# The first 512 tokens of an attention-and-MLP kernel: row norms by TensorE products, first k and v ahead of the weights

## The chip, the cores and the metric

The kernel runs on one core of a Trainium2 chip. Times are device microseconds (us) of that core; a kernel's time is the median of several executions. The engines are named TensorE (PE, with its weight loads as PEld), VectorE (DVE), ScalarE (ACT), GpSimd (POOL) and SyncE (SP). ACT, POOL and SP also issue DMAs here, each into a queue of its own.

## What is computed

Linear attention without softmax, a row norm with a gain, and an MLP with a leaky ReLU on its output. `B, H, S, D` are 8, 8, 576, 64; the MLP sees 4608 tokens of width 512 and has 2048 hidden units.

```python
kv  = np.einsum('bhsd,bhse->bhde', k, v)
out = np.einsum('bhsd,bhde->bhse', q, kv)
rms = np.sqrt(np.mean(out * out, axis=-1, keepdims=True) + 1e-06)
x   = (out / rms * g_norm)        # then (B,H,S,D) -> (B*S, H*D)
h   = x @ w_in
g   = np.maximum(0.01 * h, h)
y   = g @ w_out
```

q, k, v and g_norm are float32; the two weight matrices arrive as 64-bit floats and are rounded to float32 on the chip.

## The kernel before, in words

The tokens are cut into nine blocks of 512 (`NT`). `x` is held transposed, features on the partitions: `x[:, 2*l + e, :]` is a tile of 128 partitions by 512 tokens, and a head's 64 features are spread over two halves `e` of 32 partitions (`E`). Four groups of 32 partitions (`NP`) are the four head pairs `p`, and `l` picks one of the two heads of a pair.

The first block is made by `first_attention` and worked off by `first_block`; the other eight blocks run later with products that save multiplications (`strassen`, `product_h`, `product_o`), which the change doesn't touch.

*Loads.* `load_first` issues q, k and v of the first batch: one DMA of 288 KB for each head pair of each, through the queues "a" (ACT), "s" (SP) and "g" (POOL). Some of them land in the buffers `pairs` and `early`, which are used for something else later. Each of the 32 weight jobs (`load_w`) brings 0.5 MB of 64-bit floats into one of seven raw buffers (three in `stage`, four in `pairs`): a `w_in` job is four DMAs of 128 KB, a `w_out` job is one of 512 KB. Job 0 goes through POOL's queue, all others through SP's. After it POOL issues four small DMAs for the gain `g_sb`. A queue issues in order: a DMA that waits for a buffer or for its semaphore (eight are used in turn) holds back what stands behind it.

*Rounding.* `round_f64` (L201) takes two instructions on ScalarE (L214 "add", L216 "cut") and four on VectorE (L217, L220, L221, L223), all on 128x512. Job 0 is the first slice of `w_in`; jobs 1 and 2 are the next of `w_in` and the first of `w_out`.

*first_attention* (L391): q is turned by small products with `ident` (q_ps, rest_ps) and copied to `qT` by ScalarE and VectorE; `attention_kv` makes k-transposed-times-v in two groups of head pairs, m = 0 (pairs 0 and 1) and m = 1 (pairs 2 and 3), 36 products each; `copy_kv` moves the result to SBUF. `keep_warm` issues products of zeros whose result nobody reads. Then the 512 tokens are done in two halves of 256. For each half, `outputs` makes 16 products into PSUM tiles `o_ps`, squares them on ScalarE, adds the two halves `e` on VectorE, and writes `x` with the gain (ScalarE, L317). `divide` (L326) sums the squares over 32 partitions and spreads the root's inverse again over them: VectorE turns 32x32 squares (L331), reduces (L332), ScalarE takes the root (L334), VectorE the reciprocal (L335), ScalarE repeats each value 32 times (L338), VectorE turns back (L341) and multiplies `x` (L343). Between the halves stand four keep_warm products. Afterwards jobs 1 to 4 are rounded.

*first_block* (L747): for each of 16 slices of 128 hidden units (n = 0 to 15), four products of 128x512 make `h_ps` (for n = 0 in two halves of 256 tokens), ScalarE's leaky ReLU (L765) makes `g`, and four products add to the output sums `o_acc`; the h products of n + 1 run ahead of the o products of n. Between them `between` loads and rounds further jobs and takes steps of the next batch's attention.

The instructions that carry `pin` stay in the order in which they are written; every matmul goes through L112, and every load of q, k, v here through L124, of the weights through L192.

Of the kernel before, what the change touches and what calls it, by code (L numbers as in the profile page):

```python
# [9 lines left out]
F32 = mybir.dt.float32  # L10
U32 = mybir.dt.uint32
I64 = mybir.dt.int64
# [11 lines left out]
def kernel(  # L24
# [36 lines left out]
    nc = tc.nc  # L61
# [37 lines left out]
    def view(t, lo, *shape):  # L99
        n = 1  # L100
        for d in shape:
            n *= d
        t = t[:, lo:lo + n]
        names = "abcd"[:len(shape)]
        return t.rearrange(f"p ({' '.join(names)}) -> p {' '.join(names)}",
                           **dict(zip(names, shape))) if len(shape) > 1 else t
# [4 lines left out]
    def matmul(*args, **kw):  # L111
        pin(nc.tensor.matmul(*args, **kw))  # L112
# [4 lines left out]
    def half_of(p, i):  # L117


        return i ^ (p & 1)  # L120
# [23 lines left out]
    def load_first():  # L144

        early = xpool.tile([P, NE * NT], F32, tag="xT", name="early")
        n = J * D

        def rows(t):
            return t[:, :n].rearrange("p (j d) -> p j d", j=J)  # L150

        ks, vs = ([in_tile(name) for _ in range(2)] for name in ("k", "v"))
        qs = [rows(ins.tile([P, T * D], F32, tag="q_in", name="q_in")) for _ in range(2)]
        qs += [rows(early[:, i * n:]) for i in range(2)]
        ks, vs = (t + [pair(i + j, J, D) for i in range(2)] for j, t in ((0, ks), (2, vs)))
        for way, to, src, ts, p in (
                ("a", q_ins, q, qs, 0), ("s", q_ins, q, qs, 1), ("a", q_ins, q, qs, 2),
                ("s", q_ins, q, qs, 3), ("a", k_ins, k, ks, 0), ("s", v_ins, v, vs, 0),
                ("a", k_ins, k, ks, 1), ("s", v_ins, v, vs, 1), ("g", k_ins, k, ks, 2),
                ("g", v_ins, v, vs, 2), ("s", k_ins, k, ks, 3), ("s", v_ins, v, vs, 3)):  # L160
            to[0, p] = load_two({"a": nc.scalar, "s": nc.sync, "g": nc.gpsimd}[way],
                                src[0, 2 * p:2 * p + 2], ts[p])

    kvs = [consts.tile([P, NP, D], F32, name=f"kv_{i}") for i in range(2)]
    zeros = view(g_all[0], 0, NT)
    load_first()
    nc.vector.memset(zeros, 0.0)

# [30 lines left out]
    def round_f64(dst, raw):  # L201

        a, n = dst.shape[1:]
        lo, hi = raw[:, :, 0], raw[:, :, 1]
        add = spare(a * n, "add", U32)
        pin(nc.scalar.activation(add, lo, func=AF.Copy, scale=2.0 ** -29))  # L214
        cut = spare(a * n, "cut")
        pin(nc.scalar.activation(cut, hi.bitcast(F32), func=AF.Copy, scale=2.0 ** -112))  # L216
        pin(nc.vector.tensor_scalar(cut, cut, HIGH_MOST, -HIGH_MOST, op0=ALU.min, op1=ALU.max))  # L217
        dst = dst.bitcast(U32)
        add, cut = (t.rearrange("p (a n) -> p a n", a=a) for t in (add, cut.bitcast(U32)))
        pin(nc.vector.tensor_scalar(dst, cut, 3, None, op0=ALU.logical_shift_left))  # L220
        pin(nc.vector.scalar_tensor_tensor(dst, in0=cut, scalar=0x80000000, in1=dst,  # L221
                                           op0=ALU.bitwise_and, op1=ALU.bitwise_or))
        pin(nc.vector.tensor_tensor(dst, dst, add, op=ALU.add))  # L223

    w_in_e = w_in.rearrange("(p t i) f -> p i t f", p=NP, i=E)
# [11 lines left out]
    def load_w(j, eng=nc.sync):  # L237
# [3 lines left out]
        else:  # L241
            load(dst, src, eng)

    def round_w(j):
        if w_in.dtype == I64:
            round_f64(w_jobs[j][0], w_raws.pop(j))

    eps_sb = consts.tile([P, 1], F32, name="eps_sb")
    nc.vector.memset(eps_sb, EPS)
    warm = consts.tile([P, 1], F32, name="warm")  # L250
    nc.scalar.activation(warm, eps_sb, func=AF.Sqrt)
    ident = consts.tile([P, P], F32, name="ident")
    nc.gpsimd.memset(ident, 1.0)
    nc.gpsimd.affine_select(ident, ident, pattern=[[-1, P]], base=0, channel_multiplier=1,
                            compare_op=ALU.is_equal, fill=0.0)
    load_w(0, nc.gpsimd)
    g_sb = consts.tile([P, 2], F32, name="g_sb")
    for p in range(NP):
        pin(nc.gpsimd.dma_start(g_sb[p * E:(p + 1) * E], g_norm.rearrange("(e i) -> i e", i=E)))


    xTs = {}
# [8 lines left out]
    def attention_kv(b, m, kv_ps):  # L271

        two = [(k_ins.pop((b, p)), v_ins.pop((b, p)), p) for p in (2 * m, 2 * m + 1)]
        for j in range(J):
            for i in range(2):
                for k_in, v_in, p in two:
                    r, c = 64 * i, 64 * half_of(p, i)
                    matmul(kv_ps[p % 2][c:c + 64, m, :], lhsT=k_in[r:r + 64, j, :],
                           rhs=v_in[r:r + 64, j, :], start=(j == 0), stop=(j == J - 1))
# [12 lines left out]
    def x_of(lo, hi):  # L292
        return block(lo // NT)[:, :, lo % NT:lo % NT + hi - lo]

    def outputs(b, lo, hi, e, sums, new_ps, new=t2k, later=None):


        x, n = x_of(lo, hi), hi - lo
        o_ps = [new_ps(n, "o_ps") for _ in range(2)]
        for p in range(NP):  # L300
            for l in range(2):
                r = slice(64 * l, 64 * l + 64)
                matmul(o_ps[half_of(p, l)][E * p:E * p + E, :], lhsT=kvs[b % 2][r, p, E * e:E * e + E],
                       rhs=qTs[b][r, p, lo - b * S:hi - b * S], start=True, stop=True)
        for l in range(2):
            sq = new(n, "sq" if e else f"sum{l}")
            act = nc.scalar.activation(sq, o_ps[l], func=AF.Square)
            if later is not None:
                pin(act)
            if e == 0:  # L310
                sums.append(sq)
            else:
                nc.vector.tensor_add(sums[l], sums[l], sq)

        def keep():
            for l in range(2):
                act = nc.scalar.activation(x[:, 2 * l + e, :], o_ps[l], func=AF.Copy,  # L317
                                           scale=g_sb[:, e:e + 1])
                if later is not None:
                    pin(act)  # L320
        if later is None:
            keep()
        else:
            later.append(keep)

    def divide(lo, hi, sums, new=t2k):  # L326
        x, n = x_of(lo, hi), hi - lo
        rms = work.tile([P, 2, n // E], F32, tag="rms", name="rms", bufs=2)
        for l in range(2):
            t = new(n, "turned")  # L330
            nc.vector.transpose(t, sums[l])  # L331
            nc.vector.tensor_reduce(rms[:, l, :], t.rearrange("p (a i) -> p a i", i=E),  # L332
                                    axis=AX.X, op=ALU.add)
        nc.scalar.activation(rms, rms, func=AF.Sqrt, scale=1.0 / D, bias=eps_sb)  # L334
        nc.vector.reciprocal(rms, rms)  # L335
        for l in range(2):
            t = new(n, "spread")
            nc.scalar.copy(t.rearrange("p (a i) -> p a i", i=E),  # L338
                           rms[:, l, :].unsqueeze(2).to_broadcast([P, n // E, E]))
            inv = new(n, "inv")  # L340
            nc.vector.transpose(inv, t)  # L341
            to = x[:, 2 * l:2 * l + 2, :]
            nc.vector.tensor_mul(to, to, inv.unsqueeze(1).to_broadcast([P, 2, n]))  # L343

    def att_ps(n, name):
        return ps_att.tile([P, n], F32, tag="att", name=name)

    def tail_of(b, lo, hi):
        sums = []
        for e in range(2):  # L350
            outputs(b, lo, hi, e, sums, att_ps)
            yield
        divide(lo, hi, sums)
        yield
# [36 lines left out]
    def first_attention():  # L391
# [4 lines left out]
        def keep_warm(n=1):  # L396
            for _ in range(n):
                matmul(idle, lhsT=zeros[:, :P], rhs=zeros, start=True, stop=True)
# [19 lines left out]
        for i in range(2):  # L418
            nc.vector.tensor_copy(
                qT.rearrange("p a (t j) -> p a t j", j=J)[:, i::2, :, J - 1], rest[i])  # L420
        for m in range(2):
            attention_kv(0, m, kv_ps)
            if m == 0:
                keep_warm()
        copy_kv(0, kv_ps)
        for j in range(3, 7):
            load_w(j)
        round_w(0)
        free = iter(("ha", "hb", "hc", "oa", "hd", "oc", "ha", "hb"))

        def ps(n, name):
            return ps_m.tile([P, n], F32, tag=next(free), name=name)

        sums, later = ([], []), []
        for e in range(2):
            outputs(0, 0, N2, e, sums[0], ps, spare, later)
        for keep in later:
            keep()
        outputs(0, N2, NT, 0, sums[1], ps, spare)
        divide(0, N2, sums[0], spare)  # L440
        outputs(0, N2, NT, 1, sums[1], ps, spare)

        idle = att_ps(NT, "idle_ps")
        keep_warm(4)
        divide(N2, NT, sums[1], spare)
        for j in range(1, 5):
            round_w(j)

# [450 lines left out]
```

## Time and profile before

| what | value |
|---|---|
| median of 6 executions | 942.69 us (941.35 to 944.72) |
| the profiled execution | 941.35 us, its span 939.6 us |
| granted TensorE clock, mean | 0.997 |
| DMA | 200.03 MB, mean 213 GB/s |
| first product of zeros; first q product; first kv product | 1.53; 5.24; 9.97 us |
| first square; first h product (half the tokens); first full-width h product | 20.34; 26.72; 34.50 us |
| ScalarE square of 128x256; ReLU of 128x512 | 0.39 to 0.41; 0.60 us |
| VectorE turn, reduction, product with x (128x256, 128x256, 128x512) | 0.42; 0.39; 0.66 us |

The page's first part gives each engine's busy time and share. The second cuts the span into 40 slices of 23.5 us, too coarse for a change that lies within the first 35 us; so the timeline (instructions in order of time), the chain of waits and tables of one microsecond each are read for that stretch. A TensorE product of f32 is recorded as two matmuls. The span leaves out what lies around the program's own work: here 1.75 us.

### The profile page before, as it was taken

To read this page: it belongs to the slowest core of one execution; us is meant where nothing else is said; L and a number is where in the kernel's file an instruction comes from. 1 tells how busy PE (TensorE), PEld (TensorE's weight loads), DVE (VectorE), ACT (ScalarE), POOL (GpSimd) and SP (SyncE) were. 2 spreads that over 40 slices of the span, in tenths; PEclk is the share of its full clock that TensorE was granted. 3 is DMA by queue.
4 is the path that set the end of the run, shared out by engine and by line. 5 is a ranking of instruction groups with operands and counts; after the bars stand their busy time and mean duration, and the time that the engine had idled before them with its cause. 6 is when DMAs were issued, how large, how long until landed. Compare 5 with 4: busy or idle time off the path is not lost.

```text
span 939.6 us, 17607 instructions
## 1 busy us (share of the span) xinstructions
PE 918.6 (98%) x6878; PEld 769.8 (82%) x6878; DVE 600.1 (64%) x1001; ACT 330.8 (35%) x671; POOL 319.4 (34%) x320
## 2 busy tenths in 40 slices
PE   7899999999999999999999999999999999999997
PEld 4444446878988899889998999899988999999996
DVE  3876895678357755597547855785568755554554
ACT  3643633242134422442234323432344233223321
POOL 2000253977622352216211722263224522532222
PEclk9999999999999999999999999999999999999999
DMA  8999925985498568955896678857855665567632
GB/s 248 218 247 224 252 75 164 328 270 173 159 309 268 163 186 260 308 182 179 247 306 202 185 257 259 250 169 219 271 177 175 198 218 183 182 195 221 188 112 90
DMA packets 89810, 200.03 MB, mean 213 GB/s; under 512 B 9856, under 2 KB 41600, under 8 KB 89728
## 3 DMA queue, kind: packets, MB, share of 16 engines
q1 hardware_dynamic: 79392, 187.17, 66.2%
q10 hardware_dynamic: 9856, 10.62, 3.5%
q8 instruction: 55, 0.90, 0.4%
q0 software_dynamic: 480, 1.12, 0.4%
q14 instruction: 27, 0.22, 0.1%
HBM read 172.39 MB, written 26.48 MB: 212 GB/s over the span
## 4 chain that ended last, share of the span: by engine, by line
PE 87%; DVE 7%; DMA 3%; ACT 2%; issue 1%; SPq 0%; ACTq 0%; DVEq 0%
PE o_a L112 21%; PE o_c L112 16%; PE h_ha L112 10%; PE h_hc L112 8%; PE h_hb L112 7%; PE h_hd L112 6%; PE o_acc L112 5%; PE h_ps L112 5%; PE h_a L112 3%; DVE g L451 2%; PE h_c L112 2%; PE o_ps L112 2%; PE kv_ps L112 2%; DMA pairs<-in_v_dram 1%; DVE o L451 1%
## 5 line engine op out<-in xcount | busy, mean ns | idle before, releaser
L451 POOL TENSOR_TENSOR gs<-g 128x512 f32<-128x512 f32 x64 | 80.3, 1274 | 450.4 <-ACT g L623 450.4
L451 DVE TENSOR_TENSOR o<-o_c,o 128x512 f32<-128x512 f32 x88 | 60.5, 688 | 111.8 <-PE o_c L112 107.8
L112 PE MATMUL o_a<-pairs,gs 128*128 128x256 f32 x512 | 121.1, 379 | 0.0
L451 DVE TENSOR_TENSOR o<-o_a,o 128x512 f32<-128x512 f32 x104 | 71.1, 684 | 77.2 <-PE o_a L112 77.2
L687 ACT COPY w_all<-h_ha 128x512 f32<-128x512 f32 x84 | 48.8, 581 | 200.6 <-PE h_ha L112 200.4
L623 ACT ACTIVATE g<-g 128x512 f32<-128x512 f32 x124 | 77.4, 631 | 99.9 <-DVE g L451 97.4
L112 PEld LDWEIGHTS o_a<-pairs,gs 128*128 128x128 f32 x512 | 93.0, 190 | 10.3
L112 PE MATMUL o_a<-w,g 128*128 128x256 f32 x256 | 61.0, 381 | 3.8 <-DVE o L451 3.6
L112 PEld LDWEIGHTS h_ha<-stage,w_all 128*128 128x128 f32 x448 | 58.0, 191 | 7.0 <-issue 2.4
L112 PE MATMUL h_ps<-xT,w_all 128*128 128x512 f32 (+1 forms) x136 | 58.3, 571 | 3.9 <-DVE xT L343 3.0
L112 PE MATMUL o_c<-w,g 128*128 128x256 f32 x256 | 60.5, 379 | 0.0
L112 PE MATMUL o_c<-pairs,gs 128*128 128x256 f32 x256 | 60.5, 379 | 0.0
L112 PE MATMUL o_c<-w,gs 128*128 128x256 f32 x256 | 60.5, 379 | 0.0
L112 PE MATMUL o_a<-pairs,g 128*128 128x256 f32 x256 | 60.5, 379 | 0.0
L112 PE MATMUL h_ha<-stage,w_all 128*128 128x128 f32 x448 | 60.1, 277 | 0.0
L112 PE MATMUL o_acc<-w,g 128*128 128x512 f32 x128 | 58.0, 597 | 0.0
L112 PEld LDWEIGHTS o_a<-w,g 128*128 128x128 f32 x256 | 46.4, 190 | 10.1 <-DVE o L451 3.5
L451 POOL TENSOR_TENSOR pairs<-w_all 128x512 f32<-128x512 f32 x8 | 10.5, 1314 | 126.2 <-DMA stage<-in_moe_w_out_dram 95.2
L112 PEld LDWEIGHTS h_ps<-xT,w_all 128*128 128x128 f32 x136 | 25.3, 190 | 33.6 <-issue 26.3
L451 DVE TENSOR_TENSOR g<-g,pairs 128x512 f32<-128x512 f32 x84 | 52.8, 682 | 0.0
L451 DVE TENSOR_TENSOR w_all<-h_hc,w_all 128x512 f32<-128x512 f32 x56 | 38.4, 686 | 21.7 <-PE h_hc L112 18.5
L112 PEld LDWEIGHTS o_c<-w,gs 128*128 128x128 f32 x256 | 46.5, 190 | 5.2
(152 smaller groups left out, 1977.2 us busy)
## 6 DMA issues: line engine op xcount, KB each, us to landing
w_all<-w SPq DMA_DIRECT2D x196, 448.0 KB, 4.0
pairs<-w SPq DMA_DIRECT2D x56, 512.0 KB, 4.4
out_dram<-o ACTq DMA_DIRECT2D x36, 256.0 KB, 2.9
v_in<-in_v_dram SPq DMA_DIRECT2D x30, 288.0 KB, 6.7
k_in<-in_k_dram SPq DMA_DIRECT2D x28, 288.0 KB, 6.0
q_in<-in_q_dram SPq DMA_DIRECT2D x56, 144.0 KB, 6.2
q_in<-in_q_dram SPq DMA_DIRECT2D x56, 140.0 KB, 5.9
w<-stage SPq DMA_DIRECT2D x12, 512.0 KB, 3.5
```

What stands on the lines that cost most here:

```text
L112: pin(nc.tensor.matmul(*args, **kw))
L451: ins = eng.tensor_tensor(out_, a, b_, op=ALU.subtract if minus else ALU.add)
L623: nc.scalar.activation(t, t if src is None else src, func=AF.Prelu, alpha=SLOPE)
L687: nc.scalar.copy(q[:, at], banks[tag])
```

## The change

- The order of the first loads and their queues. k and v of pair 1 move from ACT and SP to POOL; k of pair 3 moves from SP to ACT; `ident` is made between POOL's two pairs of loads. The four `g_sb` DMAs move from POOL to SP.
- `round_f64` becomes a generator, and job 0's four VectorE instructions are issued between others.
- One keep_warm product now stands ahead of each group of kv products; the four later ones are gone.
- For the first 512 tokens `outputs` and `divide` are replaced. All 32 `o_ps` products are issued together; a square covers 128x512 (both `e`). The sum over partitions is a product: the squares are the weights (128 tokens at a time), and the moving operand is `group`, 128x4, the identity summed over groups of 32 columns. It gives tokens on the partitions. ScalarE takes the root, VectorE the reciprocal, and a second product spreads it: the weights are one column of the roots repeated 32 times, the moving operand is `ident`; the result `inv_ps` stays in PSUM, and VectorE multiplies `x` by it. The first half's products with the gain move from ScalarE to VectorE.
- The tokens 512 to 575 of the first batch and all later batches keep the old way (`tail_of`).

```diff
-                ("a", k_ins, k, ks, 1), ("s", v_ins, v, vs, 1), ("g", k_ins, k, ks, 2),
-                ("g", v_ins, v, vs, 2), ("s", k_ins, k, ks, 3), ("s", v_ins, v, vs, 3)):
+                ("g", k_ins, k, ks, 1), ("g", v_ins, v, vs, 1), ("a", k_ins, k, ks, 3),
+                ("s", v_ins, v, vs, 3), ("g", k_ins, k, ks, 2), ("g", v_ins, v, vs, 2)):
+            if (way, p) == ("g", 2) and src is k:
+                make_ident()
...
+    group = consts.tile([P, NP], F32, name="group")
+    nc.vector.tensor_reduce(group, ident.rearrange("p (a i) -> p a i", i=E), axis=AX.X, op=ALU.add)
     load_w(0, nc.gpsimd)
...
-        pin(nc.gpsimd.dma_start(g_sb[p * E:(p + 1) * E], g_norm.rearrange("(e i) -> i e", i=E)))
+        pin(nc.sync.dma_start(g_sb[p * E:(p + 1) * E], g_norm.rearrange("(e i) -> i e", i=E)))
...
         for m in range(2):
+            keep_warm()
             attention_kv(0, m, kv_ps)
-            if m == 0:
-                keep_warm()
-        copy_kv(0, kv_ps)
         for j in range(3, 7):
             load_w(j)
-        round_w(0)
...
-        for e in range(2):
-            outputs(0, 0, N2, e, sums[0], ps, spare, later)
-        for keep in later:
-            keep()
-        outputs(0, N2, NT, 0, sums[1], ps, spare)
-        divide(0, N2, sums[0], spare)
-        outputs(0, N2, NT, 1, sums[1], ps, spare)
-
-        idle = att_ps(NT, "idle_ps")
-        keep_warm(4)
-        divide(N2, NT, sums[1], spare)
+        w0 = rounding(0)
+        next(w0, None)
+        copy_kv(0, kv_ps)
...
+        def add_up(half, l):
+            for e in range(2):
+                for t in range(2):
+                    matmul(sum_ps[half][:, t, l, :], lhsT=squares[half][l][:, e, t * P:t * P + P],
+                           rhs=group, start=(l == e == t == 0), stop=(e == 1),
+                           skip_group_check=True)
...
+        def spread(half):
+            for l in range(2):
+                for t in range(2):
+                    for p in range(NP):
+                        matmul(inv_ps[half][E * p:E * p + E, l, t * P:t * P + P],
+                               lhsT=roots[half][:, t, l, p:p + 1].to_broadcast([P, E]),
+                               rhs=ident, start=True, stop=True)
...
+        for l in range(2):
+            square(0, l)
+            keep(0, l)
+            add_up(0, l)
+        next(w0, None)
+        next(w0, None)
+        square(1, 0)
+        add_up(1, 0)
+        root(0)
+        invert(0)
+        for _ in w0:
+            pass
+        square(1, 1)
+        spread(0)
+        add_up(1, 1)
+        keep(1, 0)
+        root(1)
+        keep(1, 1)
+        scale(0, 0)
+        invert(1)
+        scale(0, 1)
+        spread(1)
+        for l in range(2):
+            scale(1, l)
         for j in range(1, 5):
             round_w(j)
```

## The prediction

> **What bounds the kernel now.** I read the page's head and its chain first. TensorE is the bound:
>
> ```profile
> span 939.6 us, 17607 instructions
> PE 918.6 (98%) x6878; PEld 769.8 (82%) x6878; DVE 600.1 (64%) x1001; ACT 330.8 (35%) x671; POOL 319.4 (34%) x320
> PE 87%; DVE 7%; DMA 3%; ACT 2%; issue 1%; SPq 0%; ACTq 0%; DVEq 0%
> ```
>
> TensorE (PE) stands idle for 939.6 - 918.6 = 21.0 us in all. The table of windows of one microsecond each puts 10.6 us of that into the first 40 us (29.4 us busy), and shows it busy for all of 40 to 100 us. So the change can win only ahead of the place where the unbroken stream begins, and what it wins there moves all that follows. The chain of waits over the first 60 us gives that place (start, length, what):
>
> ```profile
> 5.00 12.62 DMA pairs<-in_v_dram
> 17.76 1.32 PE kv_ps L112 x70
> ...
> 20.34 0.46 ACT sum L307 x2
> ...
> 33.76 0.70 DVE w_all L223
> 34.50 3.70 PE h_ps L112 x8
> 38.20 3.43 PE o_acc L112 x8
> ```
>
> Three stretches are to be seen: k and v until 17.62 us; norm and scaling from the first square at 20.34; and at 34.50 the second hidden product (n = 1 of first_block), from which no gap is left. My whole sum is "where does the after-kernel start that product?". Then the timeline, for what the stretches contain (start, length, engine, line, operation):
>
> ```profile
> 13.64 2.19 PE L112 MATMUL kv_ps<-v_in,k_in 64*64 64x64 f32 x70 [3.35 <-DMA k_in<-in_k_dram]
> 15.45 0.66 ACT L214 ACTIVATE add<-stage 128x512 uint32<-128x512 uint32 x1 [5.24 <-DMA stage<-in_moe_w_in_dram]
> 19.50 1.62 PE L112 MATMUL o_ps<-qT,kv 64*32 64x256 f32 x48 [0.47 <-DVE kv L283]
> 22.92 3.70 PE L112 MATMUL idle_ps<-g 128*128 128x512 f32 x8
> 31.65 1.99 PE L112 MATMUL h_ps<-xT,w_all 128*128 128x256 f32 x8 [2.96 <-DVE xT L343]
> ```
>
> ScalarE (ACT) could begin weight job 0 only at 15.45, when its last quarter had landed; and an f32 product leaves two records (x8 is four products). Last, the DMA issues (KB each, median us from issue to landing; the x1 rows and the narrower windows give single ones):
>
> ```profile
> pairs<-in_k_dram POOLq DMA_DIRECT2D x1, 288.0 KB, 6.1
> pairs<-in_v_dram POOLq DMA_DIRECT2D x1, 288.0 KB, 7.5
> pairs<-in_v_dram SPq DMA_DIRECT2D x1, 288.0 KB, 12.6
> stage<-in_moe_w_in_dram POOLq DMA_DIRECT2D x4, 128.0 KB, 8.5
> ```
>
> With the issue times of the timeline: the POOL queue's k and v landed at 1.35 + 6.1 = 7.45 and 2.06 + 7.5 = 9.55, job 0's quarters behind them at 10.3, 11.7, 13.6 and 15.3; the last v from SP at 17.6. The windows' GB/s add up to 3.42 MB by 12 us, 3.97 by 14, 4.48 by 16, 4.72 by 17 and 5.04 by 18 (q, k, v are 3.54 MB, jobs 0, 1 and 2 are 0.5 each: exactly all of it).
>
> **The change, part by part.** *Queues.* All k and v are now issued ahead of weights: POOL has k1, v1, k2, v2 and then job 0; ACT ends with k3, SP with v3. SP's job 1 waits, quarter by quarter, for k0, v0, k3, v3 (a DMA waits for the eighth before it on its semaphore), which holds it back. Pair 1 lands where POOL's pair did, 9.55. Then 2.1 us for each 288 KB (9.55 - 7.45, three queues sharing) gives v2 at 13.75 at most; by bytes 3.54 MB are through at 12.5 at least. I take 13.3, nearer to the row of its own queue; before: 17.6.
>
> *What is late next* is job 0, now behind k2 and v2 on POOL, while its add and cut (L214, L216: 15.45 to 16.66, 1.2 us) still stand ahead of the first square in ScalarE's order. Lower bound: 3.54 + 0.5 MB, 14.2 us by the sums above. Upper: four quarters at 1.7 us (13.6 to 15.3) after 13.3, 20.1. Job 1 and some of job 2 share the engines: with job 1 whole and 0.18 MB of job 2 the bytes are 4.72 MB, so 17.0, which I take. Squares then start at 17.0 + 1.2 = 18.2. The other input is ready sooner: kv products 1.44 after v2 (17.62 to 19.06), then 0.44 to the first o_ps, then 32 records at 1.62/48 = 0.034 us: 13.3 + 1.44 + 0.44 + 1.1 = 16.3. Squares at 18.2 against 20.34: 2.1 us won.
>
> *Moved with it.* The four g_sb DMAs go from POOL to SP, where the rows for an issue are 0.33 to 0.47 us; they stand ahead of job 1, which waits for k0 (9.95) anyway, and their data, queued behind v3, is wanted only at about 19: hidden by 6 us. The memset of zeros, ident and the new group reduction (nearest row L332, 0.39 us; between 0.1 and 0.4) run before 4 us on engines that wait for q until 7: nothing. Without that wait the reduction would cost its 0.4.
>
> *Removed.* On VectorE four sums, four transposes, four reductions and four transposes back (0.42, 0.42, 0.39, 0.42 us mean): 6.6 us; on ScalarE four spread copies (0.40); on TensorE four keep-warm products, 3.4 us that lay in a wait.
>
> *Added, in microseconds after the first square.* A 128x512 activation has 0.60 (L765) and a spacing of 0.56. A sum product loads 128x128 weights for four columns: no such row. Below lies kv's 0.019 a record (1.32/70), above h_ha's 60.1/448 = 0.134 with 128 columns; the load of the weights is alike, so I take 0.11, 0.9 for a group of four products. A spread product (32 columns of weights, 128 moving): between 0.019 and 0.134; o_ps packs 32-wide products of 256 columns at 0.034, but on half the rows; I take 0.045, so 1.45 for 16 products. A product's end trails by 0.17 (0.595 mean against 0.43 spacing). Then:
> TensorE sums until 2.4; root 0 from 2.6 to 2.95. VectorE: four keeps of 0.38 (L313's kind) from 0.6 to 2.1, cut 0.42, shift 0.43, reciprocal 0.25: 3.25; the rest of job 0, twice 0.69: 4.65. Third sums 2.4 to 3.3, spread 0 until 4.75 (visible 4.9), scale (0,0) 0.66 until 5.55, fourth sums until 5.65 (5.8), root 1 until 6.15, reciprocal 6.4, scale (0,1) 7.05. Spread 1 from 6.4 to 7.85; then h_ps of n = 0 in two halves of 8 x 0.214 = 1.7: 9.55 and 11.25. Scales (1,0), (1,1): 8.0 to 9.3, then job 1's rounding, 2.35 (32.11 to 34.46): 11.65. Both meet at 11.7. Before it was 34.50 - 20.34 = 14.2. 2.5 won.
>
> The Trainium skill, "TensorE: Matmul & The Clock Gate", part 3 on packing small matmuls, speaks against this: weight loads overlap running products only where the row groups differ, and the spread products all use all rows. By it I would price them unpacked, at the 0.134 row, and the forecast would be lost, as the third rival works out. The kv row's 0.019 holds products that share rows and differ in columns, so I side with the trace; no row shows four column groups over all rows.
>
> **Sum.** 18.2 + 11.7 = 29.9 against 34.5: 4.6 us. The profiled execution took 941.35 (span 939.6); it was the fastest of six, whose median is 942.69. So 936.75 for such an execution, and 942.69 - 4.6 = **938.1** for the median. Nothing later takes it back: ScalarE's later weight jobs find their data landed (job 8, the tightest, about 3 us early: issued 31.67, at most 7.2 to land, used 42.14), and in the changed kernel jobs 3 to 6 are issued when kv ends, 4 us sooner as well. If they came later than they are used, ReLU behind them would wait and TensorE after 3.4 us.
>
> **Rivals.** (1) *Job 0 is in time*: POOL's queue has the engines nearly to itself, squares start with o_ps at 16.3, the gain is 6.5: 936.2. For it: until 10 us nothing but 2.3 KB rows moves, at 400 GB/s. Against: job 0 lies last on its queue, and job 1 is freed when k0 lands.
> (2) *Job 0 is very late and TensorE's clock falls* (slower). The windows show the clock:
>
> ```profile
> 12.00:13.00 1.00, 0.00 (x0) 0.00 (x0) 0.00 (x0) 0.00 (x0) 0.00 (x0) 1.00 1.08 250
> 14.00:15.00 1.00, 1.00 (x51) 1.00 (x46) 0.00 (x0) 0.00 (x0) 0.00 (x0) 0.50 1.13 305
> 17.00:18.00 1.00, 0.82 (x18) 0.46 (x20) 0.00 (x0) 0.00 (x0) 0.00 (x0) 1.00 1.01 323
> ```
>
> After 3.35 us idle the clock (third figure from the right) was 0.50 until about 16.4; after 2.9 us idle (28.7 to 31.6) it stayed 1.00. The four keep-warm products are gone. o_ps ends near 17.4; sums start 1.8 after job 0 lands; a gap of 3.3 needs job 0 at 18.9 or later. From there sums, spreads and the first halves of h_ps double: the chain is about 20 instead of 11.7, and 20.1 + 20 = 40.1, 5.6 late: 948. Against it: 5.04 MB were through at 18.0 with the same engines.
> (3) *Spread products don't pack*: 0.134 a record, 4.3 us for each spread. Spread 0 ends at 7.6, spread 1 at 13.6, h_ps at 17.05; 18.2 + 17.05 = 35.25: 943.4, no gain. From 0.12 a record on the gain is gone.
>
> **How the numbers follow.** A measurement tells 0.2%, 1.9 us, from no change. Forecast 0.60, (1) 0.22, (2) 0.07, (3) 0.11. Faster: the first two, 0.82; same: (3), 0.11; slower: (2), 0.07. The bounds all at their best (v2 at 12.5, squares at 15.5, chain 10.3) give 8.7 us won, 934.0; at their worst 20.1 + 1.2 + 17.05 = 38.4, 3.9 lost, 946.6. The range leaves out the outer ends: 935.0 to 941.5.
>
> **What would show it.** Last k or v near 13.3; ScalarE's first add near 17.0, waiting for the stage DMA; first square 18.2; spread groups of about 1.45 us; the full-width h_ps at 29.9 at clock 1.00. Wrong would be: the add starting before 15.5 (rival 1), a clock of 0.50 there (2), spreads of over 4 us (3), or a new wait of ScalarE for weights between 35 and 60 us.

## The result, and the profile after

The changed kernel's median is 939.36 us (937.42 to 943.39, 20 executions) against 943.1 (941.17 to 944.96, 43) of the kernel before in the same series: the ratio is 0.9963, with a 95% interval of 0.9955 to 0.997. It won 3.7 us of the 4.6 that were forecast. Its profiled execution took 941.71 us, 2.35 above its own median, so that page shows no gain at all, while the profile of the kernel before was its fastest of six. What separates the two executions of one kernel is itself an answer, so a second profile of the changed kernel (e1) is read beside it below.

The page of the changed kernel, head and shares of the chain:

```profile
span 940.0 us, 17770 instructions
PE 923.3 (98%) x6968; PEld 775.7 (83%) x6968; DVE 597.2 (64%) x990; ACT 327.6 (35%) x659; POOL 318.5 (34%) x318
PE 91%; DVE 6%; issue 1%; ACT 1%; DMA 1%; DVEq 0%; ACTq 0%
```

VectorE and ScalarE are on the path less than before (6% and 1% against 7% and 2%). TensorE has 4.7 us more of busy time, part of it work at half clock, as the windows below show. Its chain of waits over the first 60 us (start, length, what):

```profile
11.26 1.20 PE kv_ps L112 x71
12.46 2.98 issue
15.44 0.26 PE kv_ps L112
15.70 2.00 PE idle_ps L112 x2
17.70 2.23 PE kv_ps L112 x72
...
22.79 2.77 PE sum_ps L112 x24
25.56 1.01 PE inv_ps L112 x32
...
28.21 1.93 PE inv_ps L112 x32
30.14 7.80 PE h_ps L112 x24
37.94 3.43 PE o_acc L112 x8
```

The DMA waits of the kernel before are gone from it. In their place stands "issue": TensorE waits 2.98 us near the end of the first kv group, between its 71st and 72nd record, for nothing that a semaphore shows. The first full-width h product (record 17 of the 24) starts at 34.35, hardly sooner than the 34.50 of before. The DMA rows of the changed kernel (KB each, us from issue to landing) say that k and v are not late:

```profile
pairs<-in_v_dram POOLq DMA_DIRECT2D x1, 288.0 KB, 8.9
stage<-in_moe_w_in_dram POOLq DMA_DIRECT2D x4, 128.0 KB, 8.8
```

v of pair 2, the last in this execution, is issued at 3.71 and lands at 3.71 + 8.9 = 12.6. The timeline shows job 0, the first square and TensorE's products behind it:

```profile
15.83 0.66 ACT L223 ACTIVATE add<-stage 128x512 uint32<-128x512 uint32 x1 [5.07 <-DMA stage<-in_moe_w_in_dram]
22.03 1.57 ACT L452 ACTIVATE sq<-o_ps 128x512 f32<-128x512 f32 x3 [4.99 <-PE o_ps L112]
22.72 2.84 PE L112 MATMUL sum_ps<-group,sq 128*128 128x4 f32 x24
25.49 1.08 PE L112 MATMUL inv_ps<-ident,roots 128*32 128x128 f32 x32
28.21 1.93 PE L112 MATMUL inv_ps<-ident,roots 128*32 128x128 f32 x32 [0.65 <-DVE roots L475]
```

Job 0 is in ScalarE's hands from 15.83 and done at 17.0, 5 us before the first square, which waits for TensorE. The two spreads are the same 32 records; one takes 1.08 us, the other 1.93. The windows of one microsecond (busy share and count of PE, PEld, DVE, ACT, POOL; then TensorE's granted clock, DMA share, GB/s) show why:

```profile
25.00:26.00 1.00, 1.00 (x26) 0.98 (x29) 0.97 (x4) 1.00 (x3) 0.00 (x0) 1.00 1.10 248
29.00:30.00 1.00, 1.00 (x24) 0.64 (x16) 0.00 (x0) 1.00 (x3) 0.00 (x0) 0.50 1.11 213
```

So there are two losses that the forecast had not: a wait of TensorE for no input, and a clock of 0.50. The clock is at 0.50 from 14.5 to 21.3 and from 28.1 to 31.6 here.

### The profile page after: what moved, and what is told of

Same layout as the page of the kernel before. It is cut to its first block, busy times and chain, and to the rows that moved or that the text cites. A ratio compares the mean times of both kernels' runs of the same rounds, so it can differ in the third digit from the quotient of the medians.

```text
span 940.0 us, 17770 instructions
## 1 busy us (share of the span) xinstructions
PE 923.3 (98%) x6968; PEld 775.7 (83%) x6968; DVE 597.2 (64%) x990; ACT 327.6 (35%) x659; POOL 318.5 (34%) x318
## 4 chain that ended last, share of the span: by engine, by line
PE 91%; DVE 6%; issue 1%; ACT 1%; DMA 1%; DVEq 0%; ACTq 0%
PE o_a L112 22%; PE o_c L112 17%; PE h_ha L112 10%; PE h_hc L112 8%; PE h_hb L112 7%; PE h_hd L112 6%; PE h_ps L112 5%; PE o_acc L112 5%; PE h_a L112 3%; PE h_c L112 2%; PE kv_ps L112 2%; PE o_ps L112 2%; DVE g L520 2%; DVE o L520 1%; PE idle_ps L112 1%
## 5 line engine op out<-in xcount | busy, mean ns | idle before, releaser
L112 PEld LDWEIGHTS o_a<-w,g 128*128 128x128 f32 x256 | 46.4, 190 | 10.1 <-DVE o L520 3.5
L112 PEld LDWEIGHTS o_c<-w,g 128*128 128x128 f32 x256 | 46.5, 190 | 5.2
L112 PEld LDWEIGHTS o_c<-pairs,gs 128*128 128x128 f32 x256 | 46.5, 190 | 5.2
```

## The experiments

Each ratio is to the kernel before on the same chip. "First square" and "n = 1" (the first full-width h product) are from the profiled execution, the chain is their difference, the rest is the span less n = 1.

| kernel | median us | ratio, interval | first square | n = 1 | chain | rest |
|---|---|---|---|---|---|---|
| before | 943.1 | | 20.34 | 34.50 | 14.2 | 905.1 |
| changed | 939.36 | 0.9963 (0.9955 to 0.997) | 22.03 | 34.35 | 12.3 | 905.6 |
| e1 changed, again | 938.74 | 0.9957 (0.9944 to 0.997) | 18.86 | 31.1 | 12.3 | 905.2 |
| e2 loads alone | 940.2 | 0.9968 (0.9952 to 0.9984) | 17.90 | 32.07 | 14.2 | 904.7 |
| e3 norm alone | 943.57 | 1.0001 (0.9988 to 1.0014) | 21.04 | 36.3 | 15.3 | 905.6 |
| e4 one keep-warm less | 940.34 | 0.9972 (0.9957 to 0.9987) | 18.6 | 31.1 | 12.5 | 906.5 |
| e5 tiny products first | 941.17 | 0.9973 (0.9961 to 0.9986) | 20.67 | 33.0 | 12.3 | 904.4 |
| e6 one product more | 939.76 | 0.9958 (0.9945 to 0.9972) | 18.28 | 31.4 | 13.2 | 904.8 |
| e7 blocks of ones | 942.54 | 0.9988 (0.9978 to 0.9997) | 18.29 | 34.57 | 16.3 | 904.4 |
| e8 e5 and e7 | 943.81 | 1.0009 (1.0 to 1.0019) | 20.53 | 37.2 | 16.7 | 904.9 |
| e9 wide sums | 936.29 | 0.993 (0.9918 to 0.9943) | 18.17 | 29.30 | 11.1 | 905.2 |
| e10 inverse root | 936.17 | 0.9933 (0.9919 to 0.9946) | 20.14 | 29.68 | 9.5 | 904.4 |
| e11 norm alone, wide sums | 940.7 | 0.9968 (0.9955 to 0.9981) | 22.82 | 34.0 | 11.1 | 905.0 |
| e12 e9 with fewer loads | 939.81 | 0.9961 (0.9949 to 0.9974) | 21.14 | 32.3 | 11.1 | 906.2 |

The last column is the first reading: from n = 1 on, all fourteen executions take 904.4 to 906.5 us, while that product's own start varies from 29.3 to 37.2. So nearly all that the variants win or lose, they win or lose ahead of it.

**e1: the changed kernel, unaltered.** Expected:

> The changed kernel unaltered, for a second profile. Theory A (TensorE starves for instructions): TensorE again stands idle without a releaser near 12.5 to 15.4 us, at the same place in its own order (after some 449 records, the last of the first kv group), and a 16 KB packet of TensorE's instruction queue lands just before it goes on; ratio to before 0.995 to 0.997. Rival B (an accident of one slow execution): the second kv group starts within 0.7 us of the last k or v (12.6), first square at 17 to 18, span near 936.

Its timeline has both losses again, at other times:

```profile
10.13 1.27 PE L112 MATMUL kv_ps<-v_in,k_in 64*64 64x64 f32 x71
13.38 0.21 PE L112 MATMUL kv_ps<-v_in,k_in 64*64 64x64 f32 x1 [1.98 <-issue]
...
22.32 1.08 PE L112 MATMUL inv_ps<-ident,roots 128*32 128x128 f32 x32
...
25.04 1.93 PE L112 MATMUL inv_ps<-ident,roots 128*32 128x128 f32 x32 [0.65 <-DVE roots L475]
```

The same gap stands behind the same 71st record, 1.98 us this time, and the second spread again takes nearly twice the first. With 1 us less of waiting and only one window of 3.4 us at half clock ahead of the square instead of two, n = 1 comes 3.2 us sooner than in the first profile, and the span is 3.7 shorter.

**e2 and e3: one part each.** e2 is the kernel before with the new load order, queues and places of the keep-warm products ahead of kv; e3 is the changed kernel with the old ones:

```diff
+                ("g", k_ins, k, ks, 1), ("g", v_ins, v, vs, 1), ("a", k_ins, k, ks, 3),
+                ("s", v_ins, v, vs, 3), ("g", k_ins, k, ks, 2), ("g", v_ins, v, vs, 2)):
...
+        pin(nc.sync.dma_start(g_sb[p * E:(p + 1) * E], g_norm.rearrange("(e i) -> i e", i=E)))
```

> The load order, g_sb on SP and the keep-warm placement alone, with the old norm. Theory A: the last k or v lands at 12.6 but the stall keeps the first square near 19 to 20; gain 0.5 to 2 us, ratio 0.998 to 0.9995. Rival C (weight job 0 decides, as predicted): first square 17 to 18.3, gain 2 to 3 us, ratio 0.997 to 0.998.

> The new norm alone, with the old load order, queues and keep-warm placement. Theory A and C alike: kv ends near 19 as before, the chain from first square to the full-width h product takes 11.7 to 12.5 instead of 14.2, gain 1.5 to 2.5 us less 0.3 for the 16 more o_ps records ahead of the square; ratio 0.9975 to 0.9985. Rival D (the products only take TensorE's clock away): ratio 0.9995 or more.

e2 came out near the whole change (0.9968), more than either expectation allowed. Its first square, at 17.90, lies where rival C had it, but it waited for o_ps and not for job 0, whose cut ended at 17.1. e3 came out at nothing (1.0001): the shared expectation of a gain was missed, and rival D's ratio was met. e3's windows, columns as above:

```profile
22.00:23.00 1.00, 1.00 (x11) 1.00 (x11) 1.00 (x4) 0.62 (x2) 0.00 (x0) 1.00 1.21 207
23.00:24.00 1.00, 1.00 (x11) 1.00 (x11) 0.97 (x3) 0.26 (x2) 0.00 (x0) 1.00 0.71 276
24.00:25.00 1.00, 1.00 (x18) 0.98 (x21) 0.97 (x4) 1.00 (x4) 0.00 (x0) 0.80 1.01 323
...
33.00:34.00 1.00, 1.00 (x4) 0.77 (x3) 0.95 (x2) 0.74 (x2) 0.00 (x0) 0.50 1.02 309
```

TensorE is busy for the whole of each microsecond from 20 on, and yet its clock falls at 24.6 (0.80 is the mean of that microsecond) and stays at 0.50 until 34.8, three windows of 3.4 us. Spreads take 1.91 and 1.94 us, eight sum records 1.87, and the 24 h records 9.15 instead of 7.5. What the old norm has and the new one has not, besides the order of its steps, is four keep-warm products; e2 kept them, and in its profile the clock never fell. The new norm also has the thin products themselves; e9 tells the two apart.

**e4, e5, e6: three attempts that missed.** e4 leaves out the keep-warm product ahead of the second kv group, e5 puts 44 tiny products in place of the first of zeros, e6 adds one product of 128x512 behind the last sums:

```diff
# e4
-            keep_warm()
+            if m == 0:
+                keep_warm()
# e5
-        keep_warm(2)
+        keep_warm()
+        for i in range(44):
+            r = c = 64 * (i % 2)
+            matmul(idle[c:c + 64, :32], lhsT=zeros[r:r + 64, :64], rhs=zeros[r:r + 64, :32],
+                   start=True, stop=True)
# e6, ahead of spread(1)'s scale(0, 0)
+        matmul(inv_ps[1].rearrange("p a n -> p (a n)"), lhsT=zeros[:, :P], rhs=zeros,
+               start=True, stop=True)
```

> The changed kernel without the keep-warm product ahead of the second kv group. Theory A: after the stall that product stands on the path and costs 0.9 us at full clock, 1.7 to 2.0 at half; 1 to 2 us faster than the changed kernel, ratio to before 0.994 to 0.9955. Rival: the clock is low longer without it; 0.996 to 0.998.

> The changed kernel, but of the two products of zeros that TensorE begins with, one is replaced by 44 tiny ones, so that TensorE reaches the same count of instructions some 4 us sooner. Theory (TensorE's stall at about 12.5 us is a wait for its own next 16 KB of instructions, asked for at about the 200th record and late because data fills the DMA engines): the packet lands by about 10 us, no idle time 'issue' of over 0.5 us stands in the kv products, the first kv product of the second group starts right after the last k or v (about 12.6 to 13), the first square is at 17.0 to 17.5 instead of 18.9 (the unaltered kernel on a chip before); median 1.3 to 2 us under the changed kernel's, ratio to the kernel before about 0.994 (0.993 to 0.9955). Rival (the packet comes when the data queues run dry, whenever it is asked for): the stall only moves ahead, to the q products, the second group starts no sooner than 14.5, ratio 0.9955 to 0.997 as the changed kernel. Second rival: the stall goes, but ScalarE's add of weight job 0 (15.8) and its cut hold the first square at 17.1, so what is won is 1.8 at the most.

> The changed kernel with one product of zeros (128x512) added behind the last sums, ahead of the second spread. Theory (TensorE's clock falls to 0.50 in or after the sums and spreads because they keep the array too little busy; one full product holds it): the second spread takes 1.1 us like the first instead of 1.93, the halves of h_ps run at the clock 1.00, the first full-width h product stands 11.3 to 11.6 us after the first square instead of 12.3 to 12.5, ratio to the kernel before about 0.995 to 0.996 (1 us under the changed kernel). Rival (one product is too little, or comes too late in the window over which the clock is set): a window of 3.4 us at 0.50 stays, chain 12.3 to 12.5 or with the product's own 0.9 us longer, ratio 0.996 to 0.9975.

e4 won nothing: the gap (2.24 us) came all the same, the second kv group still took 1.98 us, and the ratio, 0.9972, is where the rival had it. e5 put the wrong thing to the test: the last record of zeros and the 88 tiny ones took 5.90 us where three records of zeros take 2.76 (e6), TensorE stayed slow until about 13 (24 q records took 1.49 us at 10.16, 26 of them 0.92 at 13.18), and the kv products began at 15.2 instead of 10.1 to 11.2. There was no gap in the kv groups, but TensorE reached the place at 13.65, 1.7 us after its instructions had landed (11.97). In e6 the clock had fallen at 23.8, ahead of the added product (24.07), which then took 2.06 us itself. It came too late to say whether it could have held the clock, and the chain was 13.2 us, as the rival had it.

**e7 and e8: sums by blocks of ones.** One 128x128 matrix with four 32x32 blocks of ones replaces sum and spread; 256 columns move; root and reciprocal then work on 128x512. e8 is e7 with e5's edit.

```diff
-                for t in range(2):
-                    matmul(sum_ps[half][:, t, l, :], lhsT=squares[half][l][:, e, t * P:t * P + P],
-                           rhs=group, start=(l == e == t == 0), stop=(e == 1),
-                           skip_group_check=True)
+                matmul(sum_ps[half][:, l, :], lhsT=blk, rhs=squares[half][l][:, e, :],
+                       start=(l == e == 0), stop=(e == 1), skip_group_check=True)
```

> The changed kernel with sums and spread in one product: a 128x128 matrix of ones in four blocks of 32 as weights, the squares (256 columns) moving; the sums come out already spread over their 32 rows, root and reciprocal then work on 128x512. Theory (4-column sums and 32-column spreads leave the array idle and let the clock fall; products of 256 columns don't): eight records of about 0.21 us for each half's sums instead of 24 short ones and a spread, clock 1.00 from the first square on, chain from the first square to the first full-width h product 10.5 to 11 us, ratio 0.994 to 0.9955. Rival (root and reciprocal on 128x512 instead of 128x16 cost ScalarE 0.6 and VectorE 0.5 to 2 us each time and put VectorE on the path): chain 12.5 or more, ratio 0.9965 to 0.998.

> The two edits before together: the early count of instructions, and sums by blocks of ones. Theory: both gains add, 17.1 for the first square and 10.7 behind it, first full-width h product at about 28 us, 6.5 us sooner than in the kernel before: ratio 0.993 (0.992 to 0.9945). Rival (one of the two is hidden behind something that the other doesn't move, such as the rounding of weight job 1 ahead of the first full-width h product): no better than the better one of the two alone.

For e7 the rival was right, and the price was above its own: 3.35 us where it had 0.5 to 2, and a ratio of 0.9988. VectorE in e7's timeline:

```profile
21.76 3.35 DVE L476 RECIPROCAL roots<-roots 128x512 f32<-128x512 f32 x1 [0.38 <-ACT roots L472]
27.50 3.35 DVE L476 RECIPROCAL roots<-roots 128x512 f32<-128x512 f32 x1
```

Two reciprocals of 3.35 us, where the changed kernel has two of 0.25 on 128x16, put VectorE on the path: the chain is 16.3 us. But in this profile the clock stayed at 1.00 through the norm, although TensorE stood idle for 2.0 and 2.6 us in it. That is the opposite of e3, and it led to e9. e8 was worse than either edit alone (1.0009), so nothing added up, as its rival had it. Its first square came at 20.53, as late as e5's, the chain was 16.7 us, and here the clock did fall, at 30.05, behind an idle time of 2.0 us. So wide products alone don't hold the clock through every gap.

**e9: the same sums, 64 columns wide.** Nothing is added and nothing taken away; each sum product moves the four columns sixteen times over, and the roots read the first four.

```diff
-        sum_ps = [ps_att.tile([P, 2, 2, NP], F32, tag="att", name="sum_ps") for _ in range(2)]
+        sum_ps = [ps_att.tile([P, 2, 2, 64], F32, tag="att", name="sum_ps") for _ in range(2)]
...
-                           rhs=group, start=(l == e == t == 0), stop=(e == 1),
+                           rhs=group.unsqueeze(1).to_broadcast([P, 16, NP]), start=(l == e == t == 0), stop=(e == 1),
...
-            pin(nc.scalar.activation(roots[half], sum_ps[half], func=AF.Sqrt, scale=1.0 / D,
+            pin(nc.scalar.activation(roots[half], sum_ps[half][:, :, :, :NP], func=AF.Sqrt,
```

> The changed kernel, but each sum product moves 64 columns (the four, sixteen times over) instead of 4; the roots read the first four. No instruction more or less. Theory (the clock falls because sums of 4 columns and spreads of 32 leave the array nearly idle over a whole window of 3.4 us): with 64 columns the clock stays 1.00 between the first square and the full-width h products, the second spread takes 1.1 us, the chain is 11.2 to 11.6 instead of 12.3 to 12.5 us, ratio 0.995 (0.994 to 0.9962). Rival (weight load and product of a record do not overlap, so a record gets 0.03 to 0.05 us longer): a group of 24 takes 3.6 to 4 us instead of 2.84, what the clock gives back is lost there, ratio 0.996 to 0.9985. Second rival (64 columns in 0.12 us are still too little): the clock falls as before, ratio as the changed kernel, 0.9955 to 0.997.

The timeline of e9:

```profile
18.88 2.89 PE L112 MATMUL sum_ps<-group,sq 128*128 128x64 f32 x24
21.71 1.08 PE L112 MATMUL inv_ps<-ident,roots 128*32 128x128 f32 x32
22.72 1.10 PE L112 MATMUL sum_ps<-group,sq 128*128 128x64 f32 x8
24.47 1.08 PE L112 MATMUL inv_ps<-ident,roots 128*32 128x128 f32 x32 [0.65 <-DVE roots L475]
25.48 7.49 PE L112 MATMUL h_ps<-xT,w_all 128*128 128x256 f32 x24
```

And one of its windows, columns as above, with the second spread's end in it:

```profile
25.00:26.00 1.00, 1.00 (x23) 0.77 (x15) 0.38 (x1) 1.00 (x3) 0.00 (x0) 1.00 1.08 251
```

The 24 sum records take 2.89 us instead of 2.84, the second spread 1.08 instead of 1.93, and the clock is 1.00 for the whole of the norm. The ratio, 0.993, lies clear of the changed kernel's interval, by 0.9963 - 0.993 = 0.0033, or 3.1 us, a little more than expected. The mean clock was 1.000 in all five executions of e9, and 0.991 to 0.998 in those of the changed kernel. Of the profiled executions, e9 has n = 1 at 29.30, e1 at 31.1 and the first one, with three windows at 0.50, at 34.35. This is what shows the cause: products that are busy with loading weights and move four columns don't hold the clock, and the same products with 64 columns do. Where between 4 and 64 the bound lies was not tried.

Not all of the 3.1 us comes from the columns. The chain is 1.2 us shorter than the changed kernel's (11.1 against 12.3); the rest lies ahead of the first square (18.17 against 18.86 and 22.03), where both kernels issue the same instructions. There e9's clock did not fall behind the gap in kv, and that of the two profiles of the changed kernel did. Whether it falls there goes with how busy TensorE was in the 3.41 us before, as the clock's own steps divide the time: 1.38 us (changed), 1.43 (e1) and 1.50 (e10), and the clock fell; 1.70 (e2), 1.76 (e9) and 1.91 (e6), and it stayed. So e9's 1.79 us of gap were short enough for the place where they fell in that division, which the edit doesn't set.

**e10: e7 without its reciprocals.** One ScalarE function gives the inverse root; the products with the gain are divided between ScalarE and VectorE.

```diff
-            pin(nc.scalar.activation(roots[half], sum_ps[half], func=AF.Sqrt, scale=1.0 / D,
-                                     bias=eps_sb))
+            pin(nc.scalar.activation(roots[half], sum_ps[half], func=AF.Abs_reciprocal_sqrt, scale=1.0,
+                                     bias=eps_sb))
```

> The kernel of e7 (sums by blocks of ones) with the root and the reciprocal of 128x512 (0.69 + 3.35 us there) replaced by one ScalarE function that gives the inverse root, and the products with the gain divided between ScalarE and VectorE. Theory (in e7 the two reciprocals of 3.35 us were the whole loss): the function takes 0.7 us, nothing else stands on VectorE, clock 1.00, chain from the first square to the first full-width h product 9.4 to 10.5 us, ratio to the kernel before 0.9935 to 0.995, the best so far. Rival (the function belongs to another table of ScalarE than square, copy and ReLU, and each change of table costs a load of over 1 us): two to four loads in the chain, 12.5 or more, ratio 0.9965 or worse.

The timeline of e10:

```profile
22.88 0.69 ACT L472 ACTIVATE roots<-sum_ps,eps_sb 128x512 f32<-128x512 f32 x1 [0.44 <-PE sum_ps L112]
25.07 3.66 PE L112 MATMUL h_ps<-xT,w_all 128*128 128x256 f32 x16
29.68 3.67 PE L112 MATMUL h_ps<-xT,w_all 128*128 128x512 f32 x8 [0.95 <-DVE w_all L236]
```

The chain is 9.5 us, the shortest, and the median level with e9's. Its profiled execution won it in spite of a clock of 0.50 ahead of the square (from 14.3 to 17.7, after the gap in kv). No load of a table stands in the chain. TensorE now waits for the rounding of job 1 (L236), the next bound.

**e11: the norm alone again, with wide sums.** e3's kernel with e9's edit.

> The kernel of e3 (new norm with the old load order) with sums that move 64 columns, as in e9. Theory (the new norm is worth its 2.5 us only while the clock holds, and wide sums hold it): clock 1.00 from the first square on, chain 11.0 to 11.5 us where e3 had 15.3 and the kernel before 14.2, first square at 20.5 to 21, ratio to the kernel before 0.9965 to 0.998 (e3: 1.0001). With e2 (loads alone, 0.9968) the two parts then add up to about e9's 0.993. Rival (the clock falls for what the late loads do, TensorE's wait for k ahead of the kv products): a window at 0.50 stays behind the first square, ratio 0.9985 to 1.001.

The chain is 11.1 us where e3 had 15.3, and the ratio 0.9968 where e3 had 1.0001. So the parts add up within their intervals: loads 0.0032, norm 0.0032, together 0.0064, and e9 with both is at 0.007. The first square was later than expected (22.82), since this execution waited for k until 15.3, and the clock was at 0.50 until 20.2.

**e12: fewer loads.** e9's kernel without two of the loads:

```diff
+            if p == 3 and src is not q:
+                to[0, p] = ks[2] if src is k else vs[2]
+                continue
```

> The kernel of e9 without the loads of k and v of pair 3, 0.59 MB less or about 1.4 us of the loads' stretch; the products of pair 3 take pair 2's data, so the first batch's heads 6 and 7 are left out of what is computed. Theory (the 16 KB of instructions that TensorE lacks at its 449th record wait behind the loads' packets): the packet starts about 1 to 1.4 us sooner, at 10 to 10.5, the idle time in the first kv group falls from 1.8 to under 1 us, the first square moves up to job 0's cut (17 at the latest), ratio to the kernel before 0.9915 (0.9905 to 0.9925). Rival (the packet comes a set time after the request, or the weights take the place of the missing loads at once): the packet starts at 11 to 12 as in e9, the idle time stays at 1.7 to 2 us, ratio 0.992 to 0.9935.

Both expectations were missed, in the direction that neither had. The timeline of e12:

```profile
10.34 1.27 PE L112 MATMUL kv_ps<-v_in,k_in 64*64 64x64 f32 x71
15.41 0.21 PE L112 MATMUL kv_ps<-v_in,k_in 64*64 64x64 f32 x1 [3.80 <-issue]
```

And its windows of the two microseconds around the start of the first kv group, columns as above:

```profile
9.00:10.00 1.00, 1.00 (x15) 0.51 (x10) 0.95 (x4) 0.65 (x2) 0.00 (x0) 1.00 0.68 189
10.00:11.00 1.00, 1.00 (x45) 0.66 (x48) 0.56 (x1) 0.00 (x0) 0.00 (x0) 1.00 0.68 177
```

The gap doubled, to 3.80 us. The trace's packets of queue q8, which brings instructions (55 packets of 16 KB; 56 in e5), give the frame. All of TensorE's instructions are counted: products, weight loads and, by the 450th, six or seven others. The 200th is where e5's expectation put the request for the next 16 KB, which no run shows:

| kernel | 200th instruction | first packet, start to landing | behind the gap (450th) | gap |
|---|---|---|---|---|
| before | 8.17 | 12.42 to 13.64 | 15.93 | none, TensorE waits for k until 13.6 |
| changed | 8.70 | 12.96 to 14.06 | 15.44 | 2.98 |
| e1 | 7.64 | 10.87 to 11.94 | 13.38 | 1.98 |
| e2 | 8.41 | 11.48 to 12.66 | 14.07 | 1.90 |
| e9 | 8.36 | 11.26 to 12.40 | 13.91 | 1.79 |
| e10 | 8.60 | 11.92 to 13.01 | 14.39 | 2.03 |
| e12 | 7.85 | 12.64 to 13.95 | 15.41 | 3.80 |

In all six rows with a gap TensorE goes on 1.4 to 1.5 us after this packet has landed; in e4, e6 and e7 it is 1.4 to 1.6. e5, which came to the place after the landing, had no gap. So the gap is the wait for that packet. What holds the packet back is open. It isn't the sum of k and v, since it came later with 0.59 MB less of them, and it isn't a set time, since from the 200th instruction it took 2.9 to 4.8 us. These are single executions: the changed kernel's own two differ by 2.1 us in the packet's start (12.96 and 10.87). And e12 didn't free the stretch that it was meant to free. From 9 to 11 us POOL's queue alone moved data, at 177 to 189 GB/s, and by the size of its packets (4.6 KB; job 0's have 4.1) it was mostly still k and v of pair 2, the last of them over at 11.46, as in e9. Taking loads from the other two queues didn't bring POOL's forward.

The Trainium skill, "Runtime: NRT & Kernel Launch", section "Instruction fetch mechanics", says that an engine's sequencer fetches its next 16 KB, 256 instructions, through a DMA queue of its own while it works on the current ones, and that the cost is "mostly hidden". The packets agree in size and number (13936 records of PE and PEld over 55 packets are 253 each). Here the first one isn't hidden: TensorE stands still for 1.8 to 3.8 us. The path loses less than that in e1 and e9, where the last k or v landed only at 13.9, about when the gap ended (13.38 and 13.91).

## Why the prediction was right, and where it was not

The direction and the time (938.1 forecast, 939.36 measured, inside 935.0 to 941.5) came out, but in part by two errors that offset each other in the time of the first square. By e1's profile the square came 0.7 us later than forecast and the chain took 0.6 more, so n = 1 stood at 31.1 where the forecast had 29.9.

- *Last k or v* at 13.3: it landed at 12.6 in the first profile (and in e10), at 13.9 in e1 and e9. The step holds; its upper bound of 13.75 was a little too low.
- *Job 0 at 17.0, the squares behind it at 18.2*: **this step failed.** The add began at 15.83 (15.87 in e1, 16.05 in e9), and the cut ended at 17.0. The first square never waited for it; in every kernel it waited for o_ps. So job 0 was nearly in time, as the first rival had it, but its 16.3 for the squares was not reached either, since TensorE lacked instructions and, in the changed kernel's two profiles, ran at half clock behind the gap. The kernel before had the same packet land at 13.64; there TensorE waited for k until 13.6, and so the one wait lay behind the other. The prediction took the k and v that it made earlier as the only thing that the kv products wait for. First squares at 18.86 (e1) and 18.17 (e9) are near 18.2 by accident.
- *Sum record 0.11, spread record 0.045*: 2.84/24 = 0.118 and 1.08/32 = 0.034. Both hold; the spreads pack as well as the o_ps row that was the nearer one, and the third rival falls. The sentence of the skill's "TensorE: Matmul & The Clock Gate", part 3, on overlapping weight loads, against which the trace was preferred, would have had them unpacked, though a table of the same part has a speedup of 2.38 for three column groups. Four column groups over all rows did overlap here.
- *Chain of 11.7 instead of 14.2*: 12.3 with the clock falling, 11.1 with the clock held (e9, e11). The sum of the parts was right to 0.6 us.
- *Keep-warm products removed at no cost, since they "lay in a wait"*: **this step failed.** The sum left out that the thin products in their place run at a clock that they don't hold themselves. The second rival saw that the clock could be missed, but made it depend on an idle gap of 3.3 us behind a late job 0; the gaps of 1.98 (e1) and 2.98 us (changed) were already enough ahead of the square. Behind it the clock fell with TensorE busy, in all six profiles with narrow sums (changed, e1, e3, e4, e5, e6). With sums of 64 or 256 columns it fell behind the first square in e8 alone, after an idle time, and not in e7, e9, e10, e11 and e12, of which the last four have no keep-warm product there either. Whether the four old products would have held the clock beside thin sums was not run. The price in the chain is 1.2 us (e9).
- *The kernel before's clock*, "0.50 until about 16.4": the window's mean of 0.66 puts the end at 16.7. Nothing in the sum hangs on it.
- *"Nothing later takes it back"*: holds. From n = 1 on, the changed kernel takes 905.2 to 905.6 us, the kernel before 905.1.

The same skill page, part 1, says that the clock follows how busy TensorE has been in free-running windows of 3.4 us, and its practical rule is to leave no idle gap of that length. The windows agree (28.1 to 31.6 in the changed kernel, 23.8 to 27.2 in e6). The rule alone would have passed e3, whose TensorE shows no idle time in the window before the fall, and the falls behind idle times of 1.98 and 2.98 us. It doesn't say that keeping busy with weight loads and four moving columns isn't enough, which e9 shows.

So with the clock held through all of it the change is worth 6.6 us (e9: 0.007 x 943.3), 3.1 more than as it stands: 1.2 of that in the chain, the rest ahead of the square. The gap in kv is in e9 as well; without it the square at 18.17 would still have had to wait for job 0's cut, which ended at 17.3, so that 0.9 us more was to be had at most.

## What to carry to other kernels

A high busy share alone doesn't keep TensorE's clock up: products with a full load of weights and a few moving columns are "busy" and still let it fall, so look at the granted clock after every group of thin products, and widen them, since up to 64 columns under the load cost almost nothing here. When a wait for data is removed, ask what else was waiting behind it, and count TensorE's instructions ahead of that place: past some 450 it needed a packet of its own here, which landed at 11.8 to 14.5 us, about when the last of k and v did. A part that shows no gain alone (e3) may have one that is taken back on the spot: here both parts were worth the same.

## What the runs showed of the hardware

- 24 sum records with 128x128 weights took 2.84 us with 4 moving columns and 2.89 with 64: 0.118 and 0.120 us each.
- TensorE's clock stayed at 1.00 in e7 with idle times of 2.0 and 2.6 us between products of 256 columns, and fell in e3 with no idle time between products of 4 columns. In e8 it fell at 30.05, after an idle time of 2.0.
- Without thin sums, the clock fell at the end of stretches of 3.41 us in which TensorE had been busy for at most 1.50 us (e10; 1.39 in e8), and stayed behind those with 1.57 (e7) or more.
- A VectorE reciprocal took 3.35 us on 128x512 and 0.25 on 128x16; ScalarE's inverse root on 128x512 took 0.69.
- Two executions of the same kernel differed by 3.7 us of span by where windows of 3.4 us at half clock fell and by when a 16 KB packet came.
